# A planned attention and mixture-of-experts kernel: TensorE transposes `kv` for two head pairs, not six, and the listed order is searched again

## The chip, the core and the metric

The kernel runs on one core of a Trainium2 chip: TensorE (PE, its weight loads PEld), VectorE (DVE), ScalarE (ACT), GpSimd (POOL), and SyncE (SP), which here only issues transfers. Matmuls write PSUM, in 8 banks of 128 partitions by 512 float32; the other engines bring results to SBUF. The metric is the device time of one execution in microseconds (us); lower is better.

## The reference, cut to what matters

```python
# linear attention: 8 batches, 8 heads, 576 positions, 64 numbers a head, 128 features
proj = einsum('bhsd,df->bhsf', x, w_phi)
proj = proj - max(abs(proj), axis=-1, keepdims=True)
phi(x) = concatenate([exp(proj), exp(-proj)], axis=-1)      # x = q, k
kv  = einsum('bhsf,bhsd->bhfd', k_p, v);  z = sum(k_p, axis=2)
num = einsum('bhsf,bhfd->bhsd', q_p, kv)
den = einsum('bhsf,bhf->bhs', q_p, z) + 1e-6
x = (num / den) laid out as (8, 576, 512)
# 4 experts on x: causal attention of 64 numbers each, the two best experts are kept
logits = x @ w_gate
q, k, v = x @ wq[e], x @ wk[e], x @ wv[e]
a = softmax(0.125 * q @ k.T, causal)
out += gate weight of e * (a @ v @ wo[e])
```

## The kernel before, in words

The 64 heads are 32 head pairs p, four to a batch b. Each unit of work is a generator that yields one step at a time: stream_k (`proj` of k, L501), stream_q (`proj` of q, L501), stream_kv (`kv` and `z`), stream_n (`den` at L740 and `num` at L751), stream_s and its helpers for batch b (q, k and v projections and output through `mm` at L294, scores L871), stream_t (`a @ v`, L1067). A string `ORDER` names, character by character, which live stream makes the next step; a string `SIDES` says whether a copy that both can do goes to ACT or DVE. So each engine's instruction order is fixed when the program is written: an engine takes its instructions strictly in that order and waits at the first one whose input is missing. The constants of `Plan` (costs in ns) served the search that found the strings; in the program itself they only decide which of the free PSUM banks a step takes.

For each pair stream_kv multiplies `ek` (the features of k) by `v_in` (16 matmuls, L642) and adds the sums over positions (L654; from pair 4 on from `zs`, which GpSimd's accumulating transfers fill), with small tail products every second pair (L607). The result stands in PSUM the wrong way round for stream_n and has to be transposed, 128 by 384 numbers. There are two ways, chosen by `KVD`:

```python
if p < KVD:
    copy(st.eng, 384, kvf..., o, ['kvt'], [kc])              # PSUM -> kvt, ACT or DVE
    for c in range(3):
        nc.tensor.transpose(ps[:, 128*c:128*c+128], kvf[...], ident)     # L665
    copy(st.eng, 384, kv[p % 2]..., ps...)                   # PSUM -> kv
else:
    nc.vector.transpose(kvt..., ps[:, 0:384])                # L673, 32x32 blocks
    for x in range(4):
        load(kvd[p % 2]...[:, :, x, :], kvt[32*x:32*x+32])   # to device memory
    load(kv[p % 2]..., kvd[p % 2]...)                        # back, blocks put in place
```

`load` issues on SP's queue (L327). The last `load` waits for the four before it, and SP, which works in order, waits with it. SP also issues the loads of `k_in`, `q_in`, `kt_in`, `vt_in`, the weights (`top`, `max` serve as their staging) and `v_in`. `v_in` has one buffer: the load for pair p waits until the L642 of pair p - 1 are done. stream_n may run for pair p when `kv` of pair p is there; `kv` has two buffers, `kvt` one. `warm` matmuls (L294) on a constant tile keep TensorE busy until the first x exists. `gates` is a DVE chain (L934 to L952) with a matmul at L961; L1000 and L1012 are wide DVE steps of the causal softmax, L1038 its sums on TensorE.

Of the kernel before, what the change touches and what calls it, by code (L numbers as in the profile page):

```python
# [68 lines left out]


ORDER = (
    r'1110049B32894DDBBDCB726C8D99E1B8DF7GD4FEHDH000C=EDBF5CBBB9DC1934DEFE==E98H2=HIHHCED168E<=A541F<77DBIFJCEAE6AHH'
    r'HIC93941HB<D<E<AGBC<===G<E9GGDAGGDCF9529<GD6GH9B48KEI13F<0;7EA6CKCECG@<<BIH<B;B8IGJE8?A@EF:AE57C7@A2J:?JHHF:18'
    r'6830ADEBDB;;;BFC6CC277GGE?LF?K@FBF2G@8::3BIHEF;;:DIH@?:5ADHIGBF7:HGH::EB;?FAEEE76C8C@CJI>IC?B0;<<<<95IE884B8FB'
    r'F9F<GHH02IEGHAB3?966B>81;A>8=8CB6EB9E99BD>A=>DABAAAB;88C8A?8841>;7CC;@G5?7EEJC>D;3;88KIJODEDDJICHBB;;;;;AF80:E'
    r'FFBCE>?EHEH;AAG:6FF?DC8DD8D;2;5C@@ACBBB8:MIJBI::<IAGIC@FBH99F869FHDB8DCECB83CFBFBC088=DFEECBC8:68I8BFF70HG7IID'
    r'CG8D?5=B<GH6C4:99B2ECMEBEJA8J9886=GJD?>778CMI<HJKI>I<I@<BG39E9C18IHE<A@=8=?E?9G8857?7?EHAJJF083882HGF8ICDHC8DD'
    r'998:C6:GJHI>?I<:JG<1J:7IGH7J:KJGD:?<<BB:BE>@C>;GIIF>L;8>GJGIIJ;8<:=8:HJGHGGJ:IF::LGGK?I=N8=5:=>@K802GQJMM>F:I<'
    r':<0CEEBK=CFE::CFDCDDCJBICDCJCE=D9;;IJHJ<ICIKFHDF4883DD<8<G<<=BBBEI=CCDCDGEFEHGE8BB8D6A8>:I<C5:@@JJ@JEECIAD6BFI'
    r':JK:9FLH9MCLCIJGDHAF9BFAHD8IHBCIE880DH=28BHCB9;ADA@@CA@C@AEL@HB=ECD9;JJBBJD<BGFC;38772J7GF88GG?K=FD<CF895?==A3'  # L80
    r'=8EB888E67FE18D@KHJ@<0E@BCB28=E9988BBDIJID8DGB8848AF<B6<6EE57:7::G=HICLHE3DJDI:::;<BJGC>HD9GHG>B>GADEAF>EEE=8D'
    r'880@C?=B:98:DAF6DIEH8G8GBD9<:::GHHG7BB?NICL5H7B6N=EE;BGC@FI;G=E9?BDJEEBA:<::MGKKDBCG:GC=CD@BIGLMGKFBJH<G:=1348'
    r'8>?EI8IHCA=B;C<<<B>B28>:8:>>>JD>DL8DCBFKJE8::C=<FKEA5G8@:<=HFJHH9<>99AM=6HD?EK==K3@88028K7CJCLFNMKD>?<F?8G887?'
    r'26I88I<AGCC?KJBG<?G=99?8F>H?>F88883AH?E9=I5=F170GIJ@EIKG<=A<DE=HE<7LDB9=<M808<;;C<C6FDCDA99<GGDJ8G@KK7DL85N2GB'
    r'38JGNMGNMHFE?GAG6F><<7:::48E:FF8F8CDFB=E:E:FIJKJ>8FCCCI89B9JIBHI>8:FDDC@D88A::EA3D7F:LFHK8:<II7PHFG?A?@KL@H=5B'
    r'KNN8:6::MPOAMAOGE;E:80:F28E241AKLIJIIFAEEB08=B>ECE8EF:;;89GHH8@@>?5HE6?HI?IHCFBE?B<<<<<GE6BDB>AC?E=CBCB?>:9;@9'
    r'JJ>>A89E=:GJGLKGJ@38087J<887F=88G8LKC:?8G?:KHL<FJH@69@9P95SADQNOQ3A8788O8OMQQPR<@NQN<MEB889ADF>HCIAJB>=99II>GD'
    r'E8<H2=CD8<FFCD7AA7888?D7FCJEA?0?812:503D4=>GA?EBI::H:<BLNELK6:ACBH6K9GAJG9A?I7I7<JH<HF??IAG?NJHIL<GM::<<E@>J28'
    r'88>FE8?A6KKGCFIJFG5MIK8;@EL;N3KPK8L:<NQNL>;:8L:84F0RP=L@:>>OPK:K:FO@KAF:::8LPMKHDFNFG:HFGLKJMK<IGGEEGE=E82CEDC'
    r'FDCC;E;D8F89::I;FL8LF=GGEC5:HN:<<=L=PDOSJBBJDE@<IBJ<DA<BEIMI?F=D9KE99AB01886OCEJGCE6IKACJAM>FDEBGLJGBHMFA@>883'  # L90
    r'@<I?FCB<DH<A888IG8875AGI7IDCMDE>IEK>C>BFCJ=<B??A?D999FFGE8GFEE3088882A8FFC<677F8GF8FA999AG6E<818248>I?EHJK7H<H'
    r'7ED5A>MFIENN>NEDFHE6HK388A<FFFC>DGG:;:99GDG;::::IHK<CJ<GFJKL??FFIKJEH8CB6I;DFKKDFJJ8:8<:::JJNMM8>57:GKBGQ6FP::'
    r'::HQRBD@3880808>E@R>K@C8HIKC=ID:HDEBFDBDBBDCADBBBHHG1<C@7875::9BCBA9C@@7AB<A64?@I;L?KA?HC?L?@IJ<G>;>F;;;==ACAB'
    r'F>DIE9KH9G9?FBBH<IFC;82=8FC73=M@D117B?B778M0;;;MJ@>JMLN>6IJBG9;=6@A>J?HCEG>6@6@@<46DEE53>G;;?>DAG;5II@:E?B=A:;'
    r'A;;797B>66660056CDF>D:B9C9DB<B9B668BA<3CB583B?A4;B@@?8;533BCB:@4A?<8=2224;B?@C;@6=2024C?64111336331D;F>DF?C5C1'
    r';CCC>?:133A?C93B5@3AD3AB39FB@C<78AA3>C?:9?3?B;=8<29@;?><?<A>><211877A;:A>=;>4;42;A3C<1=C?C>@000:8;?::>:7@75008'
    r'8;<4444=475EB<0C:007222?5>=822CF41;@18@;7?777D:9:;;;:01>679==6636800;<=B?95?04<7;761=000>6=6>><=89=54002<;<9;3'
    r'9:77674734607420224700<;02232=5722901>::509;7761008866838<8:50:97086880500100:8865857757957:996657161660005?=='
    r'90064444=A=7<71=1??119;588::276679;697672141125541121171101141311114144;;322=2:1591427717235100230553431131212'
    r'100=>45210<<0;;01168224224344034023200'  # L100
)
# [1090 lines left out]
```

## Time and profile before

| | |
|---|---|
| median of 3 runs | 585.31 us (583.77 to 586.79) |
| the profiled execution | 583.6 us, its span 581.6 us |
| PE busy | 568.9 us (98%), 7655 matmul instructions |
| PEld busy | 440.1 us (76%) |
| DVE busy | 531.6 us (91%) |
| ACT busy | 454.4 us (78%) |
| POOL busy | 287.3 us (49%) |
| moved by transfers | 69.74 MB, mean 120 GB/s |

The median is that of plain runs; the rows further down come from the profiled execution, whose time is 1.7 us under the median, and whose span leaves out 2.0 us around the first and last instruction. A float32 matmul stands in the profile as two instructions, a transpose as one. Matmuls overlap, so busy time counts overlapping ones once.

### The profile page before, as it was taken

The page shows a single profiled execution, that of the slowest core. Times are in us where ns is not written, and L with a number is a line of the kernel's source. Part 1 is how long each engine was busy: PE and PEld are TensorE (multiplying, and loading weights), DVE is VectorE, ACT ScalarE, POOL GpSimd, SP SyncE. Part 2 cuts the span into 40 slices and gives each one's busy share as a digit, 9 for nine tenths or more (in the row PEclk, how much of TensorE's full clock was granted, in tenths as well). Part 3 has the DMA queues.
Part 4 walks back from the last instruction along what each step waited for, and adds up shares of the span by engine and source line. Part 5 has one row for each costly group of instructions (what it writes and reads, how often), then busy time and mean ns, then how long its engine had stood idle before and what let it go on. Part 6 is the DMA issues. An engine that isn't in the chain of part 4 may idle for free.

```text
span 581.6 us, 19193 instructions
## 1 busy us (share of the span) xinstructions
PE 568.9 (98%) x7655; PEld 440.1 (76%) x7655; DVE 531.6 (91%) x1150; ACT 454.4 (78%) x1109; POOL 287.3 (49%) x223
## 2 busy tenths in 40 slices
...
GB/s 163 153 193 200 118 102 156 151 117 93 98 114 149 175 122 53 141 230 72 147 151 101 156 134 107 98 159 134 131 130 146 114 87 46 90 58 42 1 57 109
DMA packets 55049, 69.74 MB, mean 120 GB/s; under 512 B 29232, under 2 KB 32688, under 8 KB 54960
## 3 DMA queue, kind: packets, MB, share of 16 engines
...
q10 hardware_dynamic: 320, 0.59, 0.4%
q14 instruction: 29, 0.24, 0.1%
...
## 4 chain that ended last, share of the span: by engine, by line
PE 89%; DVE 5%; DMA 3%; ACT 2%; issue 1%; ACTq 0%; DVEq 0%; SPq 0%
PE ps_c L294 33%; PE ps_c L501 11%; PE ps_c L751 11%; PE ps_c L642 10%; PE ps_c L1067 7%; PE ps_c L871 7%; PE ps_c L740 5%; DMA v_in<-in_v_dram 2%; PE ps_c L654 2%; PE ps_c L607 2%; PE ps_c L1038 1%; DVE s L1000 1%; ACT s L303 1%; DMA q_in<-in_qt_dram 1%; DMA out_dram<-ot 0%
## 5 line engine op out<-in xcount | busy, mean ns | idle before, releaser
L713 POOL PARTITION_ALL_REDUCE mx<-u x64 | 145.7, 2299 | 66.2 <-DVE s L1000 17.1
L294 PE MATMUL ps_c<-x,qk 128*128 128x256 f32 (+1 forms) x768 | 108.0, 298 | 0.6 <-DVE yl L298 0.6
L294 PEld LDWEIGHTS ps_c<-x,qk 128*128 128x128 f32 x768 | 102.6, 189 | 4.4 <-issue 0.9
L979 POOL TENSOR_SCALAR_AFFINE_SELECT s<-s 128x256 f32<-128x256 f32 (+1 forms) x80 | 41.6, 557 | 79.5 <-ACT s L303 13.5
L305 ACT ACTIVATE ek<-ek 128x1024 f32<-128x1024 f32 x64 | 67.9, 1061 | 8.0 <-DVE ek L569 7.3
L996 POOL PARTITION_ALL_REDUCE max<-top x16 | 57.7, 3605 | 30.1 <-DVE top L992 14.4
L303 ACT COPY s<-ps_c 64x64 f32<-64x64 f32 (+4 forms) x141 | 52.9, 434 | 17.9 <-PE ps_c L871 17.6
L1000 DVE TENSOR_TENSOR s<-s,max 128x1152 f32<-128x1152 f32 (+4 forms) x80 | 65.6, 855 | 0.6 <-POOL max L996 0.6
L642 PE MATMUL ps_c<-ek,v_in 128*32 128x256 f32 x1024 | 61.7, 381 | 2.7 <-DMA v_in<-in_v_dram 2.7
L305 ACT ACTIVATE s<-s 128x384 f32<-128x384 f32 (+4 forms) x80 | 57.7, 742 | 7.4 <-DVE s L1000 7.1
L294 PE MATMUL ps_c<-yh,wo 128*128 128x256 f32 (+1 forms) x256 | 52.9, 300 | 0.0
L642 PEld LDWEIGHTS ps_c<-ek,v_in 128*32 128x32 f32 x1024 | 31.5, 110 | 25.8 <-DMA v_in<-in_v_dram 3.4
L331 POOL DMA_DIRECT2D zs<-ekt x28 | 23.6, 844 | 53.3 <-DVE zs L582 19.5
L294 PE MATMUL ps_c<-vg,x 128*128 128x260 f32 x384 | 49.0, 285 | 0.2 <-ACT s L303 0.2
L303 ACT COPY u<-ps_c 128x256 f32<-128x256 f32 (+1 forms) x107 | 40.6, 401 | 10.5 <-PE ps_c L501 9.9
L715 DVE TENSOR_TENSOR u<-u,mx 128x576 f32<-128x576 f32 x64 | 47.7, 760 | 0.4 <-POOL mx L713 0.4
L294 PEld LDWEIGHTS ps_c<-vg,x 128*128 128x128 f32 x384 | 47.1, 188 | 1.3 <-issue 0.5
L1067 PE MATMUL ps_c<-s,vs 128*32 128x320 f32 (+4 forms) x896 | 46.8, 357 | 0.0
L331 POOL DMA_DIRECT2D zs<-ek x28 | 25.4, 906 | 42.6 <-ACT ek L305 32.2
L566 DVE TENSOR_REDUCE pmax<-ps_c 128x4 f32<-128x512 f32 x64 | 42.5, 683 | 4.0 <-PE ps_c L501 3.5
L501 PE MATMUL ps_c<-q_in,wf 64*128 64x256 f32 (+1 forms) x256 | 42.9, 430 | 2.9 <-DMA q_in<-in_qt_dram 2.6
L305 ACT ACTIVATE mx<-u 128x576 f32<-128x576 f32 x64 | 43.3, 687 | 2.1 <-DVE u L715 1.8
(132 smaller groups left out, 1351.6 us busy)
## 6 DMA issues: line engine op xcount, KB each, us to landing
...
kvd<-kvt SPq DMA_DIRECT2D x104, 48.0 KB, 2.4
kv<-kvd SPq DMA_DIRECT2D x26, 192.0 KB, 2.6
...
```

The source lines that it names most:

```text
L294: nc.tensor.matmul(o, a, b, start=start, stop=stop, skip_group_check=True)
L303: nc.scalar.copy(o, i)
L305: nc.scalar.activation(o, i, func, **kw)
L331: nc.gpsimd.dma_start(o, i, accum_op=ALU.add)
L501: nc.tensor.matmul(o, a, b, start=True, stop=True, skip_group_check=True)
L642: nc.tensor.matmul(o[g, 0:2], v_in[:, 4 * h + t, k:64:2], ek[:, t, :, h, :].rearrange("p c (w f) -> p c w f", w=4), start=False, stop=t == ...
L713: nc.gpsimd.partition_all_reduce(M, U, 128, bass_isa.ReduceOp.absmax)
L715: dve(S, [uk], [mk], port=True).tensor_tensor(out=U, in0=U, in1=M, op=ALU.subtract)
L751: nc.tensor.matmul(ps[g:g + 32, 0:n], kvi[:, 2 * k + (h ^ p % 2), 32 * c:32 * c + 32], P_[h][c][:, s0:s1], start=c == 0, stop=c == 1, skip ...
L996: nc.gpsimd.partition_all_reduce(big.rearrange("p e s -> p (e s)"), top.rearrange("p e s -> p (e s)"), 128, bass_isa.ReduceOp.max)
L1000: dve(2 * (S - 128 * j), [('d', x, j)], [('max', z)], 1.11, True).tensor_tensor(out=block(s_, j, None, rows(j)), in0=block(s_, j, None, ro ...
L1067: nc.tensor.matmul(ps[r:r + 32, q0 - s0:s1 - s0], vs[:, j, 128 * g + 64 * e + k:128 * g + 64 * e + 64:2], ss[x][:, e, o + q0:o + s1], star ...
```

## The change

`KVD` goes from 6 to 2: pairs 2, 3, 4 and 5 take the second way, as pairs 6 to 31 do already. `ORDER` and `SIDES` are new strings from a new search, in which two costs of GpSimd's accumulating transfers were set to 900 and 850 ns (1220 and 700 before); those two numbers alone move no instruction.

```diff
-KVD = 6
+KVD = 2
 ORDER = (
-    r'1110049B32894DDBBDCB726C8D99E1B8DF7GD4FEHDH000C=EDBF5CBBB9DC1934DEFE==E98H2=HIHHCED168E<=A541F<77DBIFJCEAE6AHH'
+    r'11111110432949B62B87GBEFEE99BGGG8G8CED7BDFHHD4=9D9FKBCIDHBCHCED5==4398HHIEB92=DCGH=B67>KKFFKEIIFCBHB8F5F2:8B=='
...
 SIDES = (
...
-    def add_to(o, i, w, r, issue=1220, part=1):
+    def add_to(o, i, w, r, issue=900, part=1):
...
-        add_to(o[r], ekts[m % 2][r].rearrange("p c h f -> p (c h f)"), k, tk, 700, 0.5)
+        add_to(o[r], ekts[m % 2][r].rearrange("p c h f -> p (c h f)"), k, tk, 850, 0.5)
```

TensorE, around the L642 of pair 5 (`ek_108,v_in`) and the first `den` of pair 4 (L740 with `kv_118`); `q_in_105` is q of pair 5 or 7, `ps_c` a PSUM bank. Before:

```order
L501 MATMUL ps_c_70<-wf,k_in_102 128x128
L501 MATMUL ps_c_65<-q_in_105,wf 128x256
L501 MATMUL ps_c_63<-q_in_105,wf 128x256
L665 MATMUL ps_c_64<-ident,kvt 128x128 x3
L642 MATMUL ps_c_68<-ek_108,v_in 32x2x4x32 x16
L740 MATMUL ps_c_65<-mx_133,kv_118 32x288
```

The same place of the change:

```order
L751 MATMUL ps_c_64<-u_132,kv_119 32x320 x2
L501 MATMUL ps_c_66<-wf,kt_in 128x128
L501 MATMUL ps_c_70<-wf,kt_in 128x128
L501 MATMUL ps_c_65<-q_in_105,wf 128x256
L501 MATMUL ps_c_68<-q_in_105,wf 128x256
L501 MATMUL ps_c_69<-q_in_105,wf 128x320
L501 MATMUL ps_c_65<-q_in_105,wf 128x320
L642 MATMUL ps_c_63<-ek_108,v_in 32x2x4x32 x16
L740 MATMUL ps_c_66<-mx_133,kv_118 32x288
```

The three transposes ahead of the L642 are gone, and more projections of q stand there: all four of one pair, with a second group of four and the eight L740 of pair 3 further up, between the L642 of pair 4 and these.

SP's queue at the `v_in` loads of pairs 4 and 5, before (the second `v_in` row is pair 5's):

```order
L327 DMA v_in<-in_v_dram 128x512
L327 DMA k_in_102<-in_kt_dram 64x512 x2
L327 DMA q_in_105<-in_qt_dram 64x576 x2
L327 DMA q_in_104<-in_qt_dram 64x576 x2
L327 DMA v_in<-in_v_dram 128x512
L327 DMA k_in_103<-in_kt_dram 64x512 x2
```

and in the change, from the load for pair 4 to that for pair 5 and the two behind it:

```order
L327 DMA v_in<-in_v_dram 128x512
L327 DMA q_in_104<-in_qt_dram 64x576 x2
L327 DMA kv_119<-kvd_121 128x384
L327 DMA kt_in<-in_kt_dram 64x2x64 x2
L327 DMA k_in_103<-in_kt_dram 64x512 x2
L327 DMA q_in_105<-in_qt_dram 64x576 x2
L327 DMA max_156<-in_wts_dram 64x1024
L327 DMA kvd_120<-kvt 32x4x96 x4
L327 DMA v_in<-in_v_dram 128x512
L327 DMA kv_118<-kvd_120 128x384
```

The load of `v_in` for pair 5 now stands behind the four transfers that carry `kvt` of pair 4 out, and the way back of pair 4's `kv` right behind it.

DVE near the end of the program, from the start of the last L1000 group to the L1012 behind it (`s_154` are the scores of the last expert pair). Before:

```order
L1000 TENSOR_TENSOR s_154<-s_154,max_156 128x2x576
L1000 TENSOR_TENSOR s_154<-s_154,max_156 128x2x448
L1000 TENSOR_TENSOR s_154<-s_154,max_156 128x2x320
L1000 TENSOR_TENSOR s_154<-s_154,max_156 128x2x192
L1000 TENSOR_TENSOR s_154<-s_154,max_156 64x2x64
L948 SCALAR_TENSOR_TENSOR gt<-gt 128x20
L949 TENSOR_REDUCE gs<-gt 128x5
L950 TENSOR_TENSOR gs<-gs,tiny 128x5
L951 RECIPROCAL gs<-gs 128x5
L952 TENSOR_TENSOR col<-gt,gs 128x5x4
L1012 TENSOR_TENSOR max_156<-s_154 128x2x448
```

and in the change:

```order
L1000 TENSOR_TENSOR s_154<-s_154,max_156 128x2x576
L1000 TENSOR_TENSOR s_154<-s_154,max_156 128x2x448
L948 SCALAR_TENSOR_TENSOR gt<-gt 128x20
L949 TENSOR_REDUCE gs<-gt 128x5
L950 TENSOR_TENSOR gs<-gs,tiny 128x5
L951 RECIPROCAL gs<-gs 128x5
L952 TENSOR_TENSOR col<-gt,gs 128x5x4
L1000 TENSOR_TENSOR s_154<-s_154,max_156 128x2x320
L1000 TENSOR_TENSOR s_154<-s_154,max_156 128x2x192
L1000 TENSOR_TENSOR s_154<-s_154,max_156 64x2x64
L315 COPY gc<-ps_c_66 128x40
L1012 TENSOR_TENSOR max_156<-s_154 128x2x448
```

The end of the gate chain (L948 to L952) stands ahead of three of the five L1000, and a small copy has come between the last of them and the first L1012.

## Rows read from the trace of the kernel before

**Rows 1.** The page: its first line, and the chain that ended last, by engine

```profile
span 581.6 us, 19193 instructions
...
PE 89%; DVE 5%; DMA 3%; ACT 2%; issue 1%; ACTq 0%; DVEq 0%; SPq 0%
```

**Rows 2.** Waits of PE: who, for whom; us in total, times, longest

```profile
PE ps_c L642 <- DMA v_in<-in_v_dram: 2.7, 2, 2.4
PE ps_c L501 <- DMA q_in<-in_qt_dram: 2.6, 1, 2.6
...
PE ps_c L961 <- DVE col L952: 0.8, 1, 0.8
```

**Rows 3.** Timeline near the start: start us, us, engine, line

```profile
11.06 0.68 PE L294 MATMUL ps_c<-warm 128*128 128x128 bf16 x9
```

**Rows 4.** Instructions on `kvt`: ns least/median/most, first and last start us, forms

```profile
L673 DVE STREAM_TRANSPOSE kvt<-ps_c x26: 521/573/584, 74.8 to 505.8; 128x384 f32<-128x384 f32 x26
...
L665 PE MATMUL ps_c<-ident,kvt x18: 272/273/329, 17.2 to 66.7; 128*128 128x128 f32 x18
L303 ACT COPY kvt<-ps_c x4: 460/472/481, 23.5 to 64.0; 128x384 f32<-128x384 f32 x4
L315 DVE COPY kvt<-ps_c x2: 551/554/558, 16.6 to 31.6; 128x384 f32<-128x384 f32 x2
```

**Rows 5.** Timeline of PE, 40 to 60 us

```profile
42.52 0.55 PE L665 MATMUL ps_c<-ident,kvt 128*128 128x128 f32 x3
42.99 0.64 PE L751 MATMUL ps_c<-mx,kv 128*32 128x256 f32 x8
...
49.56 0.61 PE L751 MATMUL ps_c<-mx,kv 128*32 128x256 f32 x8
...
53.36 0.55 PE L665 MATMUL ps_c<-ident,kvt 128*128 128x128 f32 x3
56.30 1.94 PE L642 MATMUL ps_c<-ek,v_in 128*32 128x256 f32 x32 [2.39 <-DMA v_in<-in_v_dram]
```

**Rows 6.** Timeline of SP's queue at pair 8, 104 to 116 us

```profile
106.92 1.96 SPq L327 DMA_DIRECT2D kvd<-kvt  x4
108.92 0.43 SPq L327 DMA_DIRECT2D v_in<-in_v_dram  x1
...
112.51 0.42 SPq L327 DMA_DIRECT2D kv<-kvd  x1
```

**Rows 7.** The chain that ended last, 44 to 62 us: start us, us, what

```profile
45.14 0.97 PE ps_c L740 x16
46.11 1.17 PE ps_c L501 x8
...
49.80 6.45 DMA v_in<-in_v_dram
```

**Rows 8.** Transfers issued from 65 to 130 us: KB each, median us to landing

```profile
kvd<-kvt SPq DMA_DIRECT2D x16, 48.0 KB, 2.3
kv<-kvd SPq DMA_DIRECT2D x4, 192.0 KB, 2.4
```

**Rows 9.** Loads of `v_in` up to 120 us: issue to landing

```profile
DMA to landing us min/median/max: 3.0/3.5/6.4
```

**Rows 10.** Busy time by stretch: us; engines with (instructions), PEclk, DMA share, GB/s

```profile
20.00:40.00 20.00, 19.71 (x377) 12.84 (x369) 19.43 (x39) 19.36 (x40) 10.10 (x6) 1.00 0.72 177
40.00:60.00 20.00, 17.61 (x270) 10.36 (x262) 17.99 (x37) 18.12 (x42) 13.79 (x9) 1.00 0.90 201
```

**Rows 11.** Timeline near the end, DVE and PE

```profile
559.48 3.76 DVE L1000 TENSOR_TENSOR s<-s,max 128x1152 f32<-128x1152 f32 x5
...
564.34 0.41 PE L961 MATMUL ps_c<-col,ident 128*32 128x10 f32 x29 [0.82 <-DVE col L952]
...
566.07 0.95 DVE L1012 TENSOR_TENSOR max<-max,s 128x384 f32<-128x384 f32 x2
...
567.40 0.35 PE L1038 MATMUL ps_c<-max,ones 128*32 128x224 f32 x1
```

More of the change, by code (lines that the diff above doesn't have):

```diff
@@ L71 @@
 ORDER = (
-    r'1110049B32894DDBBDCB726C8D99E1B8DF7GD4FEHDH000C=EDBF5CBBB9DC1934DEFE==E98H2=HIHHCED168E<=A541F<77DBIFJCEAE6AHH'
[L73 to L100, printed above, removed]
+    r'11111110432949B62B87GBEFEE99BGGG8G8CED7BDFHHD4=9D9FKBCIDHBCHCED5==4398HHIEB92=DCGH=B67>KKFFKEIIFCBHB8F5F2:8B=='
@@ new lines @@
+    r'FFC>>3::GB7GB5B=HBGEHF1DD=G==B=:2:4F70FCB52==>=GFII9GF=:26EFBF==8G=EE4EFGDH1GE0=D86==99;JF@@D77E;;DAH@GE8G;DAD'
+    r'E84@3FFG;;@E2F1<<3:;E@<;ABHII@BBIB;68ACBFDKA;ECGE;;FGCA0AED:7GFCC;;67K3IG:HD?917CHF2:CC?F??FD;DGD648IAC=:DAGB@'
+    r':5IAIGHH96FF?9<<D<<F<FAE93>EDE99F98C099A<6E?DDB:FE:99<C8CCEEJ>:@?C9BDD8B;5HF7G7AGJGHFI;>;FBIKNFB6GHFH:G@BGBCFF'
+    r'F;;2BC;;;;I=FEFE48?1A88883200GFFFB=@CA?A::88E=D@6B;A8@C5;;:G@BIB>LICID::B>>99>KABEGH>C8C@G@@8388088>EF69G8FAJ?'
+    r'8GEHH8GGG:<GG5C767HME99<MNLCIHIAMMJ938MH8D>BJJK778ML8288?<?D>I>I<K<?@EF99>9J8>BFG<>@8GEH757IBH>DDE>EEADI99GD02'
@@ new lines @@
+    r'488D81K>8F8=:E<6J<>::=<KDJ:EIG8D67<HGC=KJD=HIH430CA:<:;EE;:BH8GFH<H<GL<HFFF87HL3ED:8DHD:J:M5AJ:N=:8KEK@?@I8888'
+    r'A:;>HELRO2N?EEDQEG=DLHK=:FGIHI::CC==>FIIAAFAFGAB;9;H<CFHIGFHCF<<:<IF<C8DBHBH8:CBF>MFBD6KCGFIBDB8:DD:5MKBLJBNHB'
+    r'OOKJJB<AAC:99E<01HD8GOLKMHB296GHGB;N8G03HHIICELCB=HBHDF88BBDFBFBDGGFDBG9ABAA;LJ9@@8;JB=IEIH7HIDJ7=??HKI?B2A<88'
+    r'C8E39875J>8>LK8887D@HJEMHIJMLHC@F<GE9E<BH?8G88968HHDD5HIHGHJFFC:77FB<=JH<F;:::::D6OAN<8KJ96OGF?HH0DG81488K32H8'
+    r'8:6@HIIBFHIBHFFGFED9B8:BB:KED9?E<EGJ8JFAE:8D?I7CKH:7IHD?5B@QQEGFKKMJG6@EAB6DDJCD;9GJ:I?;:CH<;C:GIML<CF@EJBB::G'
@@ new lines @@
+    r'BB@IKBLGMJE?FEGHE<<<DC8=320<4FFH==C>A>888>IFD>C8B8:8>8C:B:5:JD<@NNJFCCEE999:G838288JEFHB<7FFG10@BE<8??BLGIEFJ8'
+    r'@D88>>FCEBBG>IG67D8@D@FC<GCHA@?99@EKB?E39>8H0C8?A88FH8CH=5IG277A<N>OK?>I>IDGLGNGHB@@D>9N8=<HADEBCC<GB;99HKJ<@6'
+    r'I;8ED?DE75F87KNNFKJ<::::FKF01H6GGFH;:JG<B>BELHJ48388:88>DLDHD22?HHBAGFE:89HG8E@D9DFA<>DBDB:D:E>HH88:HDHE:7GDHG'
+    r'J5GGH67=8N==AD?D:>BHFHFD:K:E=:B:KG0340288818GC9KLDJEA?CKJAABEC?CCHI>:BH8;8CI3EE@8;G5KH<KJ?==D6@HDF<?CGFF?6F??D'
+    r'B<<<AG<FF:99H9HC888FI@:KLJ>LK:78QIJPM8;888:FKII6DK8<D7THRAJO99?ANO=9H8388OOL80=25F?7A4DDII=MJD6LQ@N8PIC=GKIJI8'
@@ new lines @@
+    r'99?8LE@>IDB=H?E8=?HG<=977EDG=7A2I5CMECCFIC1L:C8JAAK3A=::::<ILBKMN6IFLK=EHBAIB997AH8807<=JGJAAIIFK<88<:<?G===LN'
+    r'MIGK<EJ<F<888>?D?L86RSM5RS;TRGQ8SI=>PHCK@?FMM;::::N8A8340NO:PQPD=HON:E:F:JMG=J::IKEG6MCJM=H8281D?DBDIE;DAHFDIF'
+    r'DEEDGEDDDDEF8:;=;EEBGF98G=H8FE6:H:KK5:O:<H=PJCCCCCD<<3R=XRMTFB?<QGDDFS=QBB<RMPC0DG<A@JIMMLMCCAACL99KOH==8P0JO8'
+    r'8>NF8;J9K8@LIB@@88KD8JL=H=5K787AA@B@JD><GJE<ID23JBC999@888EJIIJ>>82>48@8F<<GH6?@GAA8>JAFIFHD8?999F77@DF>@AMBC>'
+    r'E<7FHFFK>576MMCIJBD<<CDCCB9:I9;;:GLOMN388820CO6M:8:D@:PLKCKELEILM::JED81J<DJGJD>IC>86GIFGI<8G8E8:F=I:MII:5K::<'
@@ new lines @@
+    r':;KGO=F@NQ8038828:4NFIJFFJJG:C:A6>@LHEGEG>=7EGGDDE?>CEF@:C9BBBC?GH?BCBEEB;B;C888756CF@HE8EDKKB:<@GEPEAA<<ALPGN'
+    r'<HDPG<=FIB@?A:JBDPLH@<NJM:;:GCIDFGBFA?F93098?LBH?J=>Q817;AL<KLD;AK77J@HB77>B@IA@01FA;67>>CE<F56B@F5F34F::BEGG;'
+    r'C@JI<B>B7@77CH<F66666J;A<0;<CGFH:EC0?9BB656<9C5888AA6>>B?9B4>BAB5G45@B?3?A2AD13===A?:2@26FD=H1?953CF39:011333:'
+    r'??>>5D?1AB83E138=C@@A?9@:153A33A?533C<CH<>AE9;=35AF0@98<A22?:2A=9@B=<<==<6;A7@?<@?0;0;<;;;>611321>@99=?>3<<004'
+    r'4C?;:9B99<4:9045??4::::@<00?0595=78060284222@B5<A8>6<=679=;917171=>?55535:00=6<?>0005<=86<:73960006>?565=:=:=='
@@ L101 @@
+    r'6=905903748:99239876222855350353323:220000003>=664<7<:93941710505:90010446:5>496338:806000697943:;666666576765'
+    r'343343135332130003<?0?<400??;39>:1<;1197963157998575526673532111111111322446543434366353:941229673852142331000'
+    r'2242554242420061963>?>>>22==24072377453040336403200'
 )
 SIDES = (
-    r'11110000111111000000001000011100000000110101100000001010001000000010010000110000000000000010000000000000000000'
-    r'00000000000000010000000000000000000000000000000000000000001000000000000000101001001000000000100000000000000000'
```

8 lines of the change are left out of this document (5 added, 3 removed).

## The prediction

> **What bounds the kernel now.** I read the page first, then TensorE's own waits, then the first 60 us by stretch, because the pairs concerned (2 to 5) are worked on there. The chain that ended last is 89% PE [rows 1], so TensorE's instruction stream is the kernel: the time is the work in that stream, plus what it waits. The reader should see how little the waits are: of 581.6 us, 2.7 us for `v_in`, 2.6 us for the first q at the start, 0.8 us for the gate chain near the end [rows 2]. So a change can win at most the work that it takes off TensorE and a few microseconds of waits, while a new wait costs its full length. Second, look where pairs 2 to 5 live. From 20 to 40 us DVE is busy 19.43 of 20 us and ACT 19.36, and from 40 to 60 us the transfer engines are 0.90 busy, while PE shows 17.61 of 20, its one weak stretch [rows 10]. Nothing there has room: what leaves TensorE lands on resources that are as full.
>
> **The change, part by part.** The sum is made against the profiled execution, 583.6 us; the median shown is 585.31, 1.7 more, and I add that at the end.
>
> *Transposes removed, pairs 2 to 5.* Each pair has three on PE. From the first of the three to the next group is 42.52 to 42.99, 0.47 us [rows 5], with what it costs to change from one matmul shape to another. Four pairs give 1.9 us at most. At least, each transpose costs about its share of the stream without that: from the 0.55 us span of three, less the 0.273 us that one lasts [rows 4, 5], two steps take 0.28, so one step 0.14, and 12 give 1.7. But the neighbours that now meet need a change of shape themselves, so I take 1.6, with 1.2 and 1.9 as ends.
>
> *Warm-up matmuls.* Nine of them, 0.68 us at 11.06 us [rows 3], move to the start, where PE waits 2.6 us for q anyway [rows 2]; that wait hides them, and without it they would cost their 0.7 us there. Three more come later. Gain between 0 (if PE then waits for pair 0's features) and 0.6; I take 0.2.
>
> *Work moved between DVE and ACT.* Four pairs lose two copies each: of the `kvt` copies, pair 2's was on DVE (0.554 us) and the others on ACT (0.472), and the `kv` copies, which those rows do not list, I put at the same [rows 4]. They gain one L673 of 0.573 each. DVE gets 4 x 0.573 - 0.554 = 1.7 us more in a stretch where it is 97% busy; ACT gets about 3.3 less, and other copies can be moved from DVE to it. The cost is 0 if they were, 1.7 if DVE sets the pace: I take 0.2, since PE's waits for DVE in that stretch are not among its large ones.
>
> *The way over memory.* Four pairs bring 16 transfers of 48 KB and four of 192 KB. All 20 issues stand in SP's in-order queue: four issues take 1.96 us, and the way back waits for their landing and holds SP, as for pair 8, 106.92 to 112.51 us with a `v_in` and two `kt_in` issues between [rows 6]. Landing takes 2.3 and 2.4 us from 65 to 130 us [rows 8]. From 40 to 60 us I expect more, as `v_in` shows: median 3.5, but 6.4 at most [rows 9], the 6.45 at 49.80 us [rows 7]. There the kernel before has its longest wait, 2.39 us at 56.30, for pair 5's `v_in` [rows 5]: issued at once when pair 4's L642 were over (49.56, where the next group begins), due when the transposes end (53.36 + 0.47 = 53.8).
>
> In the change, that load has more time and starts later. More time: between the L642 of pairs 4 and 5 PE now does the eight L740 of pair 3 (0.97) and projections of q and of k tails that were elsewhere, in place of the transposes. A group of four q projections is 1.17 us [rows 7]; two groups and a short tail stand there instead of half a group, about 2.0 more. So 4.3 - 0.5 + 1.0 + 2.0 = 6.8 us. Later start: the load is queued behind the four `kvd` of pair 4, which wait for pair 4's transpose on DVE, which waits for the sums behind those L740. So 0.97 + 0.57 + 1.96 = 3.5 us pass at least before it can be issued, where it was 0.3. With the same 6.45 us it lands 9.95 after; PE waits 9.95 - 6.8 = 3.2 us, against 2.4 before: 0.8 more. I take 1.0, as SP and DVE will not always be free at once. With the shortest landing, 3.0 [rows 9], there is no wait and 2.4 are won.
>
> *The arrival of `kv`.* Counting the groups of the new order at the durations that the timeline of before shows for them, I estimate that about 10.5, 11 and 7 us of PE's work lie between the sums of pairs 2, 3 and 4 and their first L740 (pair 4 has the L642 of pair 5 and its wait on top). The way needs 0.6 (L673), 2.0 (four issues), 2.3 to 6.4 to land, 0.4 and 2.4 to 6.4 again: 7.7 to 15.8 [rows 6, 8, 9], plus loads that stand between on SP. For pairs 2 and 3 the lower half fits. Pair 4's waits beside `v_in`. I take 0.4 in all, 0 to 4 as ends. Behind an L740 that waits, all of PE waits; what is late next is the division of that pair's x, and the first projections (L294) that need all four x of batch 0.
>
> The Trainium skill ("DMA: Bandwidth & Descriptors", section Anatomy of one DMA) gives a transfer about 2.0 us fixed plus its bytes at 436 GB/s. Estimated by that page, a 256 KB `v_in` lands in 2.6 us wherever it stands. The trace differs in this stretch: 6.45 us, so the sum goes by the trace.
>
> *Near the end.* PE waits 0.82 us for the gate chain before L961, while DVE does the five L1000 in 3.76 us [rows 11]. The last three, 1152 of 3200 columns, some 1.35 us, now come after the gate chain, so this wait goes. But the L1012 that feed L1038 come after them: they end at 566.07 + 0.95 = 567.0, and L1038 reads them at 567.40 [rows 11], so there is 0.4 us of room, and DVE's total is the same. The wait moves to L1038. Gain 0 to 0.8; I take 0.2.
>
> *The rest of the new order.* PE's stream holds the same other instructions and about as many changes of shape, so I give it 0, with 2 us each way: its small waits are found anew.
>
> The sum: -1.6 - 0.2 + 0.2 + 1.0 + 0.4 - 0.2 = -0.4, so 583.2 for a profiled execution, and 585.31 - 0.4 = **584.9 us** for the median.
>
> **Rivals.** *The early waits vanish* (faster). If `v_in` of pair 5 lands within 3.3 us of its late issue (6.8 - 3.5), the 2.4 are won: 585.3 - 1.6 - 0.2 - 2.4 - 0.2 + 0.2 + 0.4 = 581.5. For it speaks the median of 3.5 us [rows 9] and the fuller PE stream in between; against it that the transfers of this stretch only grow. The skill page of above would give this case, its 2.6 us being under 3.3.
>
> *The way over memory is late* (slower). If both legs take 5 us in the full stretch, as long as halfway from median to most for `v_in` [rows 9], pair 2's way takes 13 us and misses its 10.5 by 2.5, and pair 4 is as late behind its `v_in`, about 1 beyond it; pair 3, delayed with PE, is in time: 584.9 + 3.5 - 0.4 (taken above) = 588.0. It decides from landings of 3.8 us a leg on, where pair 2's way is 10.6. For it speaks the 0.90 share and SP's order; against it that PE's own delay early gives later pairs time.
>
> *The change does nothing to speak of elsewhere and DVE sets the pace* (within 0.5%): DVE's 1.7 in place of 0.2 gives 586.4.
>
> **How the numbers follow.** A measurement of this kernel tells 0.5%, 2.9 us, from no change: 582.4 to 588.2. My forecast (a small gain, eaten by the early stretch) has 0.43, and the DVE rival 0.09; both are within. The vanishing waits have 0.25 and end at 581.5, the late way 0.23 at 588.0. With the 2 us either way of the rest, a fifth of each of these two falls within, and the forecast's tails give about as much back. So faster 0.26, same 0.50, slower 0.24. The range reaches from 580.5 (the faster rival less half of the rest) to 589.5 (the slower one with as much); the likeliest case's own is 583 to 587.
>
> **What would show it.** L665 should count 6 and L673 30. The wait of L642 for `v_in` near 55 us should still be there, 2 to 4 us, issued behind four `kvd`. PE should wait less than 0.3 us at the last L961 and up to 1 us at the last L1038. If the `kvd` and `kv` landings before 60 us are under 3 us, the slower rival is dead. I am wrong if the `v_in` wait is gone, if an L740 of pairs 2 to 4 waits over 2 us for `kv`, or if waits of over 2 us stand at places that are not named here.

## The result and the profile after

The changed kernel takes **590.97 us** (median of 6 runs, 588.85 to 591.73) against 585.30 (6 runs, 583.77 to 586.79): a ratio of 1.0099, 95% interval 1.0081 to 1.0118. It is slower by about 1%, and above the top of the predicted range. The profiled execution took 591.4 us, 7.8 more than the 583.6 of before.

The page, its first line, the busy time of TensorE and VectorE, and the chain that ended last, which answer to [rows 1]:

```profile
span 589.6 us, 19213 instructions
...
PE 574.4 (97%) x7646; PEld 440.8 (75%) x7646; DVE 530.6 (90%) x1142; ACT 455.8 (77%) x1113; POOL 288.0 (49%) x223
...
PE 82%; DVE 7%; DMA 4%; issue 2%; POOL 2%; SPq 1%; ACT 1%; ACTq 0%; DVEq 0%; POOLq 0%
```

TensorE has 12 transposes less to do and is busy 5.5 us longer: busy time also counts matmuls that run at half the clock or are held up too briefly for the profile to call it idle; how the 5.5 us divide is not shown. Its share of the chain fell from 89% to 82%, and SyncE's queue (SPq, 1%) and GpSimd (2%) are in it now. TensorE's waits, against [rows 2]:

```profile
PE ps_c L501 <- DMA q_in<-in_qt_dram: 3.1, 2, 1.6
PE ps_c L740 <- DMA kv<-kvd: 1.3, 2, 0.9
PE ps_c L1038 <- DVE max L1012: 1.2, 1, 1.2
...
PE ps_c L871 <- DVE kvt L673: 0.9, 1, 0.9
```

The `v_in` wait of 2.4 us is gone, and so is that of L961. `q_in` was there with the 2.6 us of the start; that wait is 1.6 now, and a second of 1.4 stands at 45 us. New are `kv`, L1038 and a wait for VectorE. By stretch, against [rows 10]:

```profile
40.00:60.00 20.00, 16.64 (x214) 8.21 (x213) 15.07 (x30) 14.16 (x35) 11.53 (x9) 0.91 0.84 201
```

From 40 to 60 us all three compute engines do less than before (VectorE 15.07 for 17.99, ScalarE 14.16 for 18.12), so it is not their load that sets the pace there, and TensorE's granted clock is 0.91 in the mean where it was 1.00. TensorE's timeline in that stretch:

```profile
41.05 0.72 PE L751 MATMUL ps_c<-u,kv 128*32 128x320 f32 x8
42.64 0.69 PE L740 MATMUL ps_c<-mx,kv 128*32 128x288 f32 x8 [0.86 <-DMA kv<-kvd]
43.12 0.69 PE L740 MATMUL ps_c<-u,kv 128*32 128x288 f32 x8
45.22 0.67 PE L501 MATMUL ps_c<-q_in,wf 64*128 64x256 f32 x2 [1.40 <-DMA q_in<-in_qt_dram]
46.35 1.21 PE L501 MATMUL ps_c<-q_in,wf 64*128 64x256 f32 x6 [0.46 <-ACT u L303]
47.48 0.84 PE L607 MATMUL ps_c<-ekt,vt_in 64*32 64x256 f32 x16
48.25 1.08 PE L751 MATMUL ps_c<-mx,kv 128*32 128x256 f32 x8
49.10 1.08 PE L751 MATMUL ps_c<-u,kv 128*32 128x256 f32 x8
49.95 1.29 PE L751 MATMUL ps_c<-mx,kv 128*32 128x320 f32 x8
```

First `kv` of pair 2 is late, then `q_in` of pair 5, then, as the profile has it, a tile behind it on ScalarE. But `q_in` comes in two transfers: the second was issued at 40.93 and landed 5.3 us later, at 46.2, so the group of 46.35 could hardly have begun sooner without ScalarE. After these three waits the clock records show 1.2 GHz from 47.84 to 51.26 us: an L751 group of 320 columns takes 1.29 us where it took 0.72 at 41.05. What the last wait hangs on shows the chain that ended last (start us, us, what):

```profile
34.49 1.91 PE ps_c L642 x32
36.40 0.15 SPq L327
...
39.15 0.59 SPq L327
39.75 0.04 issue
39.79 0.58 SPq L327
40.38 0.04 issue
40.42 4.66 DMA q_in<-in_qt_dram
45.08 0.14 issue
45.22 0.68 PE ps_c L501 x2
```

For 4 us the chain is nothing but SyncE issuing one transfer behind the other, at up to 0.59 us each. The queue itself:

```profile
32.16 1.97 SPq L327 DMA_DIRECT2D kvd<-kvt  x4
34.17 0.47 SPq L327 DMA_DIRECT2D max<-in_wts_dram  x1
34.74 2.45 SPq L327 DMA_DIRECT2D k_in<-in_kt_dram  x2
37.24 2.50 SPq L327 DMA_DIRECT2D vt_in<-in_v_dram  x4
39.79 0.58 SPq L327 DMA_DIRECT2D kv<-kvd  x1
40.42 1.10 SPq L327 DMA_DIRECT2D q_in<-in_qt_dram  x2
41.62 3.62 SPq L327 DMA_DIRECT2D kvd<-kvt  x4
```

The Trainium skill ("Perfetto Trace Analysis", section What "DMA-bound" means) names this case: a kernel can be bound by the sequencer that issues, whose track is then solid with transfers being issued, which is time for making descriptors and not for moving data. The trace agrees from 36.40 to 40.38 us; the 4.66 us behind them are the transfer itself.

**Where the 7.8 us are.** Idle rows do not add up to them, so I worked out one more thing. Each group of matmuls got the duration that it has where nothing is waited for (fitted over all groups of the trace, with what a change of shape costs); summed in the order of the stream, that is 569.4 us of work before, 568.2 after. When a group really begins less the sum up to it is the time lost so far. This is an estimate; but for kernels with the same order of matmuls the differences between two rows are simply those between the starts of their L642 (pair 4: 51.68 us changed, 48.64 once more). In us, at the start of L642 of pair p, for the profiled execution of each kernel:

```
                              p=0    p=3    p=4    p=5    p=8    p=31   work
before                        1.90   2.37   2.36   4.81   5.26   6.44   569.4
changed                       3.37   3.65   8.89  10.68  13.88  14.68   568.2
changed, once more            2.92   2.87   5.85   8.66  11.89  12.63   568.2
b_kvd2: old order, new way    2.56   9.49  17.50  19.98  26.28  27.13   567.9
a_kvd6: new order, old way    3.27   4.00   4.33   7.34  10.02  10.81   569.9
a_kvd4: way from pair 4 on    2.98   3.71   4.05   6.48   8.99   9.85   569.0
a_quarter: quarter of bytes   2.58   2.46   7.24   9.03  11.16  11.91   568.2
a_onex: and fewer transfers   3.42   3.70   4.96   7.60  10.36  11.13   568.2
a_sp: two moves on SyncE      2.79   2.71   5.21   8.79  13.61  14.37   568.1
a_q: one move on SyncE        2.84   2.91   9.37  11.16  13.05  13.95   568.1
a_dve: VectorE's order        2.73   2.62   7.59   9.38  10.83  11.60   568.2
a_best: a_kvd4 and a_dve      2.92   3.71   4.05   6.17   6.86   7.88   569.0
```

Before to changed: 1.2 us less work; 1.5 more lost at the start; 5.2 between the L642 of pairs 3 and 4 (none before); 1.8 from there to pair 5, where before lost 2.5 to `v_in`; 3.2 from pair 5 to 8 (0.5 before); then hardly anything to pair 31 (0.8 against 1.2). That leaves some 0.7 for the end of the program. Nearly the whole loss is made in the first 110 us.

### The profile page after: what moved, and what is told of

Its sections match the earlier page's. It is cut to its first block, busy times and chain, and to the rows that moved or that the text cites. A ratio compares the mean times of both kernels' runs of the same rounds, so it can differ in the third digit from the quotient of the medians.

```text
span 589.6 us, 19213 instructions
## 1 busy us (share of the span) xinstructions
PE 574.4 (97%) x7646; PEld 440.8 (75%) x7646; DVE 530.6 (90%) x1142; ACT 455.8 (77%) x1113; POOL 288.0 (49%) x223
## 4 chain that ended last, share of the span: by engine, by line
PE 82%; DVE 7%; DMA 4%; issue 2%; POOL 2%; SPq 1%; ACT 1%; ACTq 0%; DVEq 0%; POOLq 0%
PE ps_c L294 30%; PE ps_c L501 11%; PE ps_c L751 9%; PE ps_c L642 9%; PE ps_c L1067 7%; PE ps_c L871 6%; PE ps_c L740 5%; DMA q_in<-in_qt_dram 1%; PE ps_c L607 1%; PE ps_c L1038 1%; DVE s L1000 1%; PE ps_c L654 1%; DMA kvd<-kvt 1%; SPq L327 1%; DVE max L1012 1%
## 5 line engine op out<-in xcount | busy, mean ns | idle before, releaser
L1000 DVE TENSOR_TENSOR s<-s,max 128x1152 f32<-128x1152 f32 (+4 forms) x80 | 62.7, 817 | 1.1 <-POOL max L996 1.1
L305 ACT ACTIVATE s<-s 128x1152 f32<-128x1152 f32 (+4 forms) x80 | 57.8, 740 | 6.9 <-DVE s L1000 5.0
L642 PE MATMUL ps_c<-ek,v_in 128*32 128x256 f32 x1024 | 61.6, 381 | 0.1
L303 ACT COPY s<-ps_c 128x256 f32<-128x256 f32 (+4 forms) x138 | 51.4, 432 | 10.2 <-PE ps_c L871 9.7
L303 ACT COPY u<-ps_c 128x320 f32<-128x320 f32 (+1 forms) x113 | 42.0, 403 | 21.9 <-PE ps_c L501 21.3
L642 PEld LDWEIGHTS ps_c<-ek,v_in 128*32 128x32 f32 x1024 | 31.4, 110 | 24.9 <-issue 4.8
L501 PE MATMUL ps_c<-q_in,wf 64*128 64x256 f32 (+1 forms) x256 | 45.8, 440 | 4.3 <-DMA q_in<-in_qt_dram 3.1
L715 DVE TENSOR_TENSOR u<-u,mx 128x576 f32<-128x576 f32 x64 | 49.7, 792 | 0.0
L751 PE MATMUL ps_c<-mx,kv 128*32 128x320 f32 (+1 forms) x512 | 44.6, 419 | 0.6 <-DVE widey L762 0.6
```

The costliest lines, as they stand in the source:

```text
L303: nc.scalar.copy(o, i)
L305: nc.scalar.activation(o, i, func, **kw)
L501: nc.tensor.matmul(o, a, b, start=True, stop=True, skip_group_check=True)
L642: nc.tensor.matmul(o[g, 0:2], v_in[:, 4 * h + t, k:64:2], ek[:, t, :, h, :].rearrange("p c (w f) -> p c w f", w=4), start=False, stop=t == ...
L715: dve(S, [uk], [mk], port=True).tensor_tensor(out=U, in0=U, in1=M, op=ALU.subtract)
L751: nc.tensor.matmul(ps[g:g + 32, 0:n], kvi[:, 2 * k + (h ^ p % 2), 32 * c:32 * c + 32], P_[h][c][:, s0:s1], start=c == 0, stop=c == 1, skip ...
```

## The experiments

All have five to twelve timed runs beside those of the kernel before, on the same chip. Theory A: the way over memory costs, through SyncE's queue and the transfer engines. Theory B: the newly searched order of the compute engines is poorer by itself.

**Order and way, crossed.** One kernel has the new order with the old way, one the old order with the new way:

```diff
 a_kvd6                                      b_kvd2
-KVD = 2                                    -KVD = 6
+KVD = 6   # ORDER: 20 SP steps become      +KVD = 2   # ORDER: 3 steps of each
+          # 3 steps for each of 4 pairs    +          # of 4 pairs become 6
```

> The changed kernel's order as it stands, but TensorE transposes kv for pairs 2 to 5 again (the VectorE transpose becomes a VectorE copy, the three TensorE transposes stand where the first 48 KB transfer stood, the copy into kv where the fourth stood; the 20 transfers of these pairs are gone). Theory A, the way over memory is what costs: the 20 transfers delay what stands behind them in SyncE's queue, so the stalls between 34 and 52 us (5.2 us against the kernel before) and between 75 and 100 us (2.5 us) go, 1.6 us of transposes come back, and the start (1.5 us) stays lost: 591.0 - 7.7 + 1.6 = 584.9, 584 to 587. Theory B, the newly searched order is poorer in itself, whatever way kv takes: the stalls stay and the transposes are added, 591 to 593.

> The order of the kernel before, not searched anew, with the way over memory for pairs 2 to 5 (VectorE transpose where the copy out of PSUM stood, the four 48 KB transfers where the TensorE transposes stood, the read of kv where the last copy stood). Theory A (the way costs): slower than before, 588 to 592, with waits for kv or for loads queued behind the new transfers between 34 and 100 us. Theory B (the order costs): 585.3 less 1.6 us of transposes, 583.5 to 585.5.

Measured: new order with the old way 589.47 us (ratio 1.0076, 1.0050 to 1.0102); old order with the new way **605.01** (1.0344, 1.0310 to 1.0378). Neither theory alone. In the first, the 5.2 us between pairs 3 and 4 shrink to 0.3, as A says, but the losses further on stay, as B says, with 1.7 us of work more. In the second, the way put into the old order as it stands costs 20 us, more than I gave it; how much of that is my own placing of its steps is not shown. Its waits of TensorE:

```profile
PE ps_c L740 <- DMA kv<-kvd: 11.5, 3, 5.4
PE ps_c L642 <- DMA v_in<-in_v_dram: 4.8, 3, 4.1
PE ps_c L501 <- DMA q_in<-in_qt_dram: 3.1, 1, 3.1
```

So the newly searched order is what makes the way bearable: it takes 14 of these 20 us back, its own costs included.

**Which pairs.** As the first, for pairs 2 and 3 alone:

```diff
-KVD = 2
+KVD = 4   # ORDER: 12 steps of pairs 2 and 3 become 6
```

> The changed kernel's order, TensorE transposes back for pairs 2 and 3 only; pairs 4 and 5 stay on the way over memory. If the loss of the way lies in the crowded stretch of 34 to 52 us alone: 0.8 us of transposes against 4 to 5 us of stalls, 587 to 589, at or under the run with transposes in all six pairs (589.5). If pairs 4 and 5 cost as much as they did in the run before (stalls of 2.5 us between 52 and 80 us in either), 589 to 590.5.

Measured: **587.35** (1.0037, 1.0022 to 1.0051). Pairs 2 and 3 on the way cost 3.6 us net of their transposes against this set of the changed kernel, 2.3 against the second one further down (589.66). Pairs 4 and 5 on it are no loss: with TensorE doing them too (a_kvd6) the time is 2.1 higher, of which 1.0 is work and 0.71 a wait for a `kvt` copy that my placement of pair 5's transposes brings in.

**Bytes or places.** The same order and instructions, with less in the transfers of pairs 2 to 5:

```diff
 # a_quarter: one of four column blocks out, 32 of 128 partitions back
-load(kvd[p % 2]...[:, :, x, :], kvt[32 * x:32 * x + 32], ...)
+load(kvd[p % 2]...[:, 0:j, x, :], kvt[32 * x:32 * x + 32, 0:j], ...)   # j = 1 if p < 6 else 4
 # a_onex: the first of the four transfers alone
+if p > 5 or x == 0: load(kvd[p % 2]...[:, :, x, :], kvt[32 * x:32 * x + 32], ...)
```

> The changed kernel, order and number of transfers untouched, but the transfers of pairs 2 to 5 carry a quarter of the bytes (one of four column blocks out, a quarter of the partitions of kv back; the rest of kv keeps what an older pair left, so those pairs' output is not the reference's). Theory A1, bytes: the memory side of the transfers, 170 to 250 GB/s between 20 and 65 us, is what the added 1.6 MB load: most of the 5.2 us between pairs 3 and 4 go, 586.5 to 589. Theory A2, places: what costs is that 20 more transfers stand in SyncE's queue and take of its eight in flight, whatever they carry: 590 to 591.5.

> As the run with a quarter of the bytes, but that quarter goes out in one transfer instead of four (the first partition block alone, and a quarter of the columns back; the rest of kv is old): 12 transfers fewer on SyncE's queue in pairs 2 to 5. Theory A1 (bytes): within 0.5 us of the run with a quarter of the bytes. Theory A2 (places in the queue): 586.5 to 589, at least 1.5 us below it.

Measured: 589.20 (1.0067, 1.0045 to 1.0089) and 588.78 (1.0055, 1.0033 to 1.0076). These are 1.8 and 2.2 us under 590.97, but 0.5 and 0.9 under the second set of the changed kernel, so the medians do not part bytes from places. The runs of a_onex scatter (585.75 to 591.23): the five with a granted clock of 0.998 or more have a median of 586.15, the six others 589.6, where the changed kernel has 589.25 and 590.9. The traces tell more. With a quarter of the bytes no L740 waits for `kv`, but `q_in` of pair 5 is still late:

```profile
41.96 0.67 PE L501 MATMUL ps_c<-q_in,wf 64*128 64x256 f32 x2 [0.41 <-ACT ekt L305]
44.77 1.59 PE L501 MATMUL ps_c<-q_in,wf 64*128 64x256 f32 x6 [2.14 <-DMA q_in<-in_qt_dram]
```

With 12 transfers fewer as well, that wait is gone and in the profiled execution the clock stays up, but the time lost is 6.9 us from pair 0 to pair 8 all the same, against 8.6: TensorE, earlier now, waits for `zs` and for VectorE.

What goes with `q_in`'s lateness in these traces is a transfer of GpSimd's, `zs<-ek` of 512 KB. The changed kernel, then a_onex:

```profile
39.80 1.06 POOL L331 DMA_DIRECT2D zs<-ek  x1 [4.22 <-DVE ekt L557]
...
39.84 1.06 POOL L331 DMA_DIRECT2D zs<-ek  x1 [4.21 <-DVE ekt L557]
38.60 1.10 SPq L327 DMA_DIRECT2D q_in<-in_qt_dram  x2
```

In the changed kernel both transfers of `q_in` are issued behind it and land after 4.7 and 5.3 us. In a_quarter the second stands 0.67 us behind it (39.28, 38.61) and takes 5.4. In a_onex both stand ahead of it and take 2.6 and 2.8. In the run a_q below it is `kv` that is issued behind it (40.25, 39.05) and takes 4.5. So a later place seems to cost not only the issues ahead, but also that the load then shares the transfer engines with `zs`. No run moved `zs` alone, so this is argued, not shown.

**Another order on SyncE.** `q_in` of pair 5 with `kv` of pair 2 behind it put ahead, and pair 5's four `kvd` put ahead of four `vt_in` and a weight at 64 us (a_sp); then `q_in` alone (a_q). The rows are SyncE's around 32 us; the second place of a_sp is not among them:

```diff
 L327 DMA kvd_120<-kvt 32x4x96 x4
+L327 DMA q_in_105<-in_qt_dram 64x576 x2      (both)
+L327 DMA kv_118<-kvd_120 128x384             (a_sp only)
 L327 DMA max_156<-in_wts_dram 64x896
 L327 DMA k_in_102<-in_kt_dram 64x512 x2
 L327 DMA vt_in<-in_v_dram 64x64 x4
-L327 DMA kv_118<-kvd_120 128x384             (a_sp only)
-L327 DMA q_in_105<-in_qt_dram 64x576 x2      (both)
```

> The changed kernel with only SyncE's order altered at two places: q_in of pair 5 and the read of kv of pair 2 are issued ahead of a weight, two k_in and four vt_in transfers (32 to 42 us), and the four transfers of pair 5 ahead of four vt_in and a weight (64 to 70 us). Theory A (what is queued on SyncE behind the added transfers lands late): the waits for kv and q_in at 42 to 46 us, the stretch at half clock after them and the wait at 79 us go or shrink: 586.5 to 589. Theory B (order of the compute engines): no wait of these was the cause, 590 to 591.5.

> The changed kernel with one move in SyncE's queue: the two q_in transfers of pair 5 are issued right behind the four transfers of pair 2, ahead of a weight, two k_in, four vt_in and the read of kv of pair 2. Theory A2 (places in the queue make q_in late, its wait lets TensorE's clock fall): q_in's wait at 45 us and the 3.4 us at half clock go, 588 to 589.5. Theory C (what is won there waits at the next late transfer, as in the run with two moves, which won 2.7 us by 48 us and had lost it by 80 us): 590 to 591.5.

Measured: 591.85 (1.0108, 1.0080 to 1.0136) and 590.88 (1.0104, 1.0082 to 1.0127): nothing won. With both ahead, 2.5 us are lost between pairs 3 and 4 instead of 5.2, and by pair 8 the loss is the old 13.6, in waits of 0.5 to 1.1 us for `kv`, `v_in` and tiles of other engines. With `q_in` alone ahead, the chain has the same shape and only another name in it:

```profile
39.61 0.59 SPq L327
40.20 0.04 issue
40.25 4.53 DMA kv<-kvd
44.77 0.14 issue
44.91 2.15 PE ps_c L740 x16
```

TensorE waits 3.88 us for `kv` there and falls to 1.2 GHz for 6.83 us. Theory C, made after a_sp, is borne out by a_q: what goes ahead puts back what stands behind it.

**TensorE's clock.** Warm-up matmuls in the waits of the changed kernel, then that kernel once more:

```diff
-pk, ps = yield Step('PE', 'c', ready)
+pk, ps = yield Step('PE', 'c', ready); fill(ps, 16 if p == 2 else 0)               # ahead of L740
-t0, t1 = yield Step('PE', 'c', ready, n=2)
+t0, t1 = yield Step('PE', 'c', ready, n=2); fill(t0[1], 44 if p == 5 and s0 == 0 else 0)   # ahead of L501
```

> The changed kernel with 60 added warm-up matmuls (128x128, on PSUM tiles about to be overwritten) where TensorE waits for kv of pair 2 (16 of them) and for q_in of pair 5 (44): they lie within waits of 0.9 and 1.4 us. If the waits only bring about the stretch at the half clock (3.4 us at 1.2 GHz), TensorE's clock stays at 2.4 GHz and half of that stretch comes back: 589 to 589.8, the waits themselves staying. If the stretch does not hang on these waits, or its work was covered by other waits: 590.5 to 592.

> The changed kernel once more, untouched, to see how far its time and the moments at which TensorE's clock rises and falls repeat from one set of executions to the next: 590.2 to 591.7, with the fall to half clock near 48 us if the waits before it bring it about, and without it if it is chance.

Measured: 590.04 (1.0088, 1.0063 to 1.0113) and 589.66 (1.0085, 1.0059 to 1.0111). Filled, all six runs have a granted clock of 0.998 or more, and the kernel is no faster for it; the time lies between the two forecasts. But the warm-up matmuls take 1.07 and 2.63 us there, longer than the waits of 0.86 and 1.40 that they were put in, so the run does not tell what the clock alone is worth. Untouched, the clock stayed up too in a_again's profile, and there `kv` of pair 2 is in time (L740 waits 0.28 us for VectorE) and `q_in` alone is late:

```profile
44.95 1.21 PE L501 MATMUL ps_c<-q_in,wf 64*128 64x256 f32 x6 [1.87 <-DMA q_in<-in_qt_dram]
```

So whether it falls is partly chance: of the changed kernel's twelve runs, seven have a mean granted clock of 0.997 or less (median 590.9 us) and five 0.998 or more (589.25): some 1.6 us apart. The two sets of the changed kernel also differ by 1.3 us, though nothing in it was altered, so that differences of that size between sets carry nothing.

**VectorE's order.** A wait that has nothing to do with the way. At 97 us, in the changed kernel:

```profile
97.23 2.36 DVE L1000 TENSOR_TENSOR s<-s,max 128x1152 f32<-128x1152 f32 x2 [0.82 <-POOL max L996]
...
99.51 0.58 DVE L673 STREAM_TRANSPOSE kvt<-ps_c 128x384 f32<-128x384 f32 x1
...
100.14 0.41 PE L871 MATMUL ps_c<-qh,kkh 64*128 64x320 f32 x1 [0.93 <-DVE kvt L673]
```

Pair 7's sums are ready at 96.85, but VectorE stands for GpSimd's maximum and then does two wide subtractions; the PSUM tile that L673 would free is the one that L871 needs.

```diff
+L673 STREAM_TRANSPOSE kvt<-ps_c_67 128x384
 L1000 TENSOR_TENSOR s_153<-s_153,max_156 128x2x576
 L1000 TENSOR_TENSOR s_153<-s_153,max_156 128x2x448
-L673 STREAM_TRANSPOSE kvt<-ps_c_67 128x384
```

> The changed kernel with one change of VectorE's order: the transpose of pair 8 is put ahead of the two subtractions of the first softmax maxima (L1000), which wait for GpSimd's maximum and hold it up at 97 to 100 us, with TensorE waiting 0.9 us for the PSUM tile behind it. Theory B (order of the compute engines): that wait is a part of the loss that has nothing to do with transfers, and it stays lost to the end: 589.7 to 590.3. If what follows is paced by another engine, no change, 590.7 to 591.3.

(It is pair 7 counted from 0, as elsewhere here.) Measured: **589.17** (1.0064, 1.0045 to 1.0084). The loss from pair 7 to 8 falls from 1.4 us to nothing and stays won to the end:

```profile
95.18 0.58 DVE L673 STREAM_TRANSPOSE kvt<-ps_c 128x384 f32<-128x384 f32 x1 [0.50 <-PE ps_c L654]
95.69 2.32 DVE L1000 TENSOR_TENSOR s<-s,max 128x1152 f32<-128x1152 f32 x2
```

The subtractions begin no later than their input allows. The medians give 1.8 us against the first set of the changed kernel and 0.5 against the second; the 1.4 rest on the trace.

**The two together, and the old kernel's own wait.**

```diff
 # a_best: a_kvd4 with the move of a_dve
 # b_fill: the kernel before, with
+if p == 5: fs = yield Step('PE', 'c'); fill(fs, 40); plan.release('c', fs)   # ahead of L642
```

> The two edits that helped most, together: TensorE transposes back for pairs 2 and 3 (587.35 by itself) and VectorE's transpose of pair 7 ahead of the two subtractions (589.17 by itself, 1.8 less than the changed kernel, of which its trace shows 1.2). If they lie in separate stretches and nothing between is shared: 587.35 - 1.2 to 1.8 = 585.5 to 586.2, the time of the kernel before. If the second only helped because of the stalls that the first removes: 587 to 588.

> The kernel before, with 40 warm-up matmuls (128x128, into a PSUM tile that is free) in TensorE's wait of 2.4 us for v_in of pair 5, and nothing else changed. In the last set of its runs, those with a mean granted clock of 0.999 or more had a median of 584.1 us, those with 0.995 to 0.997 one of 586.2. If that wait is where the clock sometimes falls: all runs at 0.998 or more and a median of 583.5 to 584.5, a version below both kernels. If the clock falls elsewhere or by chance: 585 to 586, and the split of the clocks as before.

Measured: a_best **585.65** against 585.64 for the kernel before beside it (1.0009, 0.9994 to 1.0024). The two edits add up and give back the whole loss; no more than that. b_fill 585.93 against 585.53 (1.0002, 0.9989 to 1.0016). There the first half of the expectation came true: all 12 runs have a granted clock of 0.998 or more, where 8 of the 17 runs of before had 0.996 to 0.997. The second half didn't: no time is won. In its profile L642 begins the moment the last warm-up matmul is over:

```profile
55.98 2.39 PE L465 MATMUL ps_c<-warm 128*128 128x128 bf16 x40 [0.25 <-ACT u L303]
```

`v_in` was issued at 51.35 and landed 5.8 us later, at 57.2, and the warm-up matmuls last to 58.37. So some 1.2 us of them lie behind the wait that they were to fill, and the run does not tell what the clock gives back; a smaller number wasn't tried. No version beat the kernel before.

## Why the prediction was wrong

Two steps failed. The larger by the crossed runs is *the rest of the new order*, "0, with 2 us each way": the new order with the old way (a_kvd6) is 4.5 us slower than the kernel before (589.47 against 584.98), of which 0.5 is work in changes of shape and 0.71 the wait that my placement brings in. The prediction gave a zero to waits that it had not looked for. The way adds 1.5 us to that (590.97), about what two sets of one kernel may differ by. The two do not simply add: in the old order the same way costs 20 us.

The other is the term for the way over memory, *the arrival of `kv`*, "0.4 in all, 0 to 4 as ends". Its mechanism, the way late in a full stretch, is the slower rival's, but the sum priced the wrong transfer. Pair 2's `kv` was late by about 1 us in the first profile and in time in a_again's. Behind it on SyncE stood `q_in` of pair 5, which the prediction never looked at: it counted what waits for the added transfers, not what queues behind them, except `v_in`. With pairs 2 and 3 off the way (a_kvd4) the same `q_in` is issued at 35.80 us, not at 40.42. By the sums of the table its first transfer brought 1.5 us, the tile that the profile puts to ScalarE, with the second transfer, 0.9, and the clock's fall 1.7 (half of 3.41). With `kv`'s 1.0 these make 5.1 of the 5.2 lost there (the rows call 1.40, 0.46 and 0.86 of it idle). In a_again, where the clock stayed up, the same stretch lost 3.0.

Point by point:
- *Transposes, -1.6*: right. L665 counts 6 and L673 30, as predicted (rows of `kvt`, against [rows 4]), and the summed work of a_kvd6 is 1.7 above that of the changed kernel.

```profile
L673 DVE STREAM_TRANSPOSE kvt<-ps_c x30: 539/574/584, 31.5 to 513.4; 128x384 f32<-128x384 f32 x30
...
L665 PE MATMUL ps_c<-ident,kvt x6: 272/273/329, 18.6 to 27.4; 128*128 128x128 f32 x6
```

- *Warm-up matmuls, -0.2*: wrong in sign. Pair 0's L642 begins at 14.41 us for 13.65. About 0.7 of the 1.5 us is order: in a_quarter the clock rose at 7.91 us, as before (7.92), with 2.58 lost for 1.90. The rest went with the later rise (10.30 us), which the sets show to vary.
- *Work between DVE and ACT, +0.2, and the rival that DVE sets the pace*: right to dismiss; from 40 to 60 us both did less.
- *`v_in` of pair 5, +1.0*: wrong, the wait is gone, as the faster rival said. But its 2.4 us were not won: 1.8 us go in small waits in the same stretch, so 0.7 is gained. TensorE, held up by 5 us earlier, simply came later than `v_in`, which landed 3.4 us after its late issue, where the prediction took 6.45. The formula that the prediction cites beside it stands in a section on transfers that GpSimd issues; `v_in` is SyncE's, and the sum does not use it.
- *Near the end, -0.2*: the wait did move from the last L961 to the last L1038, behind the L1012 as predicted, but it is 1.20 us there where the old one was 0.82: no gain. The rows, against [rows 11]:

```profile
566.62 2.35 DVE L1000 TENSOR_TENSOR s<-s,max 128x1152 f32<-128x1152 f32 x2
569.72 0.20 DVE L952 TENSOR_TENSOR col<-gt,gs 128x20 f32<-128x20 f32 x1
569.82 1.48 DVE L1000 TENSOR_TENSOR s<-s,max 128x640 f32<-128x640 f32 x3
...
572.60 1.81 DVE L1012 TENSOR_TENSOR max<-max,s 128x640 f32<-128x640 f32 x3
...
574.55 0.59 PE L1038 MATMUL ps_c<-max,ones 128*32 128x224 f32 x8 [1.20 <-DVE max L1012]
```

- *The rest of the new order, 0 with 2 each way*: the larger failed step, as above. Of its 4.5 us VectorE's order at 97 us is 1.2 to 1.4, shown by a_dve; the start and small waits from 52 to 80 us are read from the table, and no run altered them alone.
- *What would show it wrong*: "if the `v_in` wait is gone" was met. Of the rivals, the late way (588.0) was nearest, and its bound on the leg was fair: `kvd` from 20 to 65 us lands in 3.5 us, `kv` in 2.9. By that the rival itself would hardly have decided; what decided stood in the queue and in the rest of the order.
- *The range*: its top should be 589.0 by its own rule, 588.0 and half of the rest, not 589.5. The measured time is above either.

What stays open: what `zs<-ek` by itself does to the loads behind it, how the 3.2 us between pairs 5 and 8 divide beyond VectorE's 1.2 to 1.4 and `kv` of pair 5 (0.4 of waiting at 79.42 us), and whether the clock's fall is all of what parts the changed kernel's two medians, 590.97 and 589.66.
